# Attention and feed-forward kernel: probabilities × v in f32 for every pair of heads, and weight maxima spread over the partitions by a product with an identity

## The chip, the cores and the metric

One core of one Trainium2 chip. The metric is the device time of one execution in microseconds, of which the median over several runs is compared. TensorE is called PE here (PEld for its weight loads), VectorE DVE, ScalarE ACT, GpSimd POOL, and SP is the engine whose queue issues nearly all DMAs.

## What is computed

Shapes: 8 batches, 8 heads, 1152 keys, head dimension 64, 576 pooled queries; w_in 512×2048 and w_out 2048×512.

```python
def _attn_ref(q, k, v):
    q_pool = q.reshape(B, H, S // 2, 2, D).mean(axis=3)
    scores = scale * np.matmul(q_pool, k.transpose(0, 1, 3, 2))
    scores = scores - np.max(scores, axis=-1, keepdims=True)
    attn = np.exp(scores)
    attn = attn / (np.sum(attn, axis=-1, keepdims=True) + 1e-09)
    return np.matmul(attn, v).astype(np.float32)

def _moe_ref(x, w_in, w_out):       # x: 4608 x 512, heads side by side
    h = x @ w_in
    g = h * np.cos(h)
    return (g @ w_out).astype(np.float32)
```

q, k and v arrive as f32, the two weight matrices as f64.

## The kernel before

**Attention.** The work goes in 32 pairs of heads (`NP`; the pair number is `p` or `n`). Each pair has 9 key blocks of 128 keys (`KT`) and one remainder step, 10 units in all (`NU`). `s_unit` (L851, L871) makes the scores of a key block for both heads, 128 keys by 1024 queries, in the PSUM tile `st`, as f16 products in two parts. `soft` turns them into probabilities with one exponential on ACT. `av` and `av_mm` (L919) multiply these with v and add up in the PSUM tiles `ava` and `avb`, one for each head of the pair. The last 64 queries of both heads go through the remainder step, as products of half the array's width. The row maxima of the scores come from a product of its own (`mx`, L646 to L703), which DVE reduces (L656 and others), and the list `JOBS` loads, casts, splits and transposes q, k and v two pairs ahead of their use.

**Two ways of the product with v.** For `p < NDIR` (the first 4 pairs, which are batch 0) `soft` writes the probabilities as f32 into `pp` (L892), and `av` makes one f32 product for each of 4 query tiles and 2 heads, 8 products of 65 columns a key block. `prep_v` then writes v scaled as f32 (L768). For the other 28 pairs `soft` writes f32 `e` (L897), ACT casts it to f16 (L900), and POOL (L906) or, every third unit, DVE (L902) subtracts to get the low half; `prep_v` and `prep_v_lo` do the same to v (L772, L781). `av` then makes three products for one: high with high, high with low, low with high, 24 f16 products of 64 or 65 columns a key block. `prep_q1` casts the pooled q to f16 on ACT for `n < NDIR` (L592) and on DVE for the others (L594).

**Feed-forward.** A chunk is 256 rows. `ffn1` (L1149) and `ffn2` (L1205) do f16 products in three parts on PE; `evac`, `ew_group` and `evac2` do the cosine gate and the scaling on ACT, DVE and POOL. It starts when the weights of both layers are ready and is fed in between the attention units by a credit (`FRATE`); what is left runs after the last pair.

**Weights.** `weight_group` loads f64 columns as pairs of words (`wraw`), reduces their magnitude to one maximum a partition (`wmx`, L437), and puts f32 together (L444 to L450). The maximum over all partitions is reached by writing `wmx` to DRAM (L468, `row`), reading it back to every partition (L470, `wam`), and reducing on DVE (L477). A few small steps (L479 to L490) make a power of two of it, by which ACT and POOL scale and split the weights to f16 (L496 to L498). `weight_steps` moves the groups on, `SRATE` steps a unit.

**Order.** At the end `arrange` rebuilds the order of every engine's instructions with a list scheduler on cost estimates; each engine then runs its list strictly in that order. Matrix products of one PSUM tile are kept together as one node, to which an f32 product adds 0.3 us in its estimate.

Of the kernel before, what the change touches and what calls it, by code (L numbers as in the profile page):

```python
# [9 lines left out]
F32 = mybir.dt.float32  # L10
F16 = mybir.dt.float16
U32 = mybir.dt.uint32
I32 = mybir.dt.int32
AF = mybir.ActivationFunctionType
ALU = mybir.AluOpType
# [4 lines left out]
P = 128  # L20
POW2_MASK = 0x7F800000
POW2_HIGH = 0x40000000
TINY = 1e-12
PMAX = 2.0**6
MDIV = 64.0
VLAG = 3
# [5 lines left out]
NG = 8  # L32
# [3 lines left out]
DSH = 3  # L36
DFIRST = 0
WPOOL = 1
NDIR = 4
WLD = 2  # L40
WBN = 4
WGATE = 4
SRATE = 1.6
EWR = 2

_INS = ["q", "k", "v", "moe_w_in", "moe_w_out"]
# [80 lines left out]
def arrange(tc, nc, extra):  # L127
# [3 lines left out]
    for i in rec:  # L131
        rd, wr = boxes(i)
        eng = str(i.engine).split(".")[-1]
        if eng == "PE":
            key = wr[0][0].name
            if last_pe is not None and last_pe["key"] == key and len(last_pe["ins"]) < 12:
                nd = last_pe
            else:
                nd = last_pe = dict(eng=eng, ins=[], rd=[], wr=[], cost=0.0, lock=False, key=key)
                nd["tile"] = None  # L140
                nodes.append(nd)
            size = tuple(i.tile_size)
            c = max(n_out(wr) * 0.000421, 0.027)
            if rd[0][4] == 4:
                c = 0.3
            if size[0] == 64 and tuple(i.tile_position)[0] == 64:
                c = 0.0
            nd["cost"] += c
            nd["tile"] = size[0]
        else:  # L150
            nd = dict(eng=eng, ins=[], rd=[], wr=[], cost=0.0, lock=False)
            nodes.append(nd)
            if eng == "SP":
                nd["cost"] = 0.06
                nd["dma"], nd["lat"] = transfer(type(i).__name__, rd[0], wr[0])
            else:
                nd["cost"], nd["lock"] = estimate(i, type(i).__name__, rd, wr)
                nd["func"] = str(getattr(i, "func", "")) if eng == "Activation" else ""
        nd["ins"].append(i)
        nd["rd"] += rd  # L160
        nd["wr"] += wr
# [5 lines left out]
    for k, nd in enumerate(nodes):  # L167
        deps = set()
        for w, lst in ((0, nd["rd"]), (1, nd["wr"])):
            for t, box, *_ in lst:  # L170
                name = t.name
                if name not in hist:
                    hist[name] = ([], [], set())
                    tag = getattr(t, "tag", None)
# [72 lines left out]
    while total:  # L247
# [20 lines left out]
        c = nd["cost"]  # L268
# [43 lines left out]
def tile_attention_ffn(  # L312
# [87 lines left out]
    def all_max_end(dst, am):  # L400
        nc.vector.tensor_scalar_max(am, am, TINY)
        pow2_of(dst, am)

    w1v = w_in.rearrange("(c p) f -> p c f", p=P)
    w2v = w_out.rearrange("(f p) e -> p f e", p=P)

    w1_ready = [False]
    gate = [None]
    hsc_live = [0]

    def weight_group(wi, i0, fts):
        src, rows, width, dst = (
            (w1v, HP, DFF // NWP, w1),
            (w2v, NF, DM // NWP, w2),
        )[wi]
        n = len(fts)
        mx = sb2.tile([P, n], F32, tag="wmx", name="wmx")
        for a, ft in enumerate(fts):
            i = i0 + a
            cs = slice(i * width * WORDS, (i + 1) * width * WORDS)  # L420
            if wide:
                while hsc_live[0] >= 2:
                    yield
                hsc_live[0] += 1
                raw = sb2.tile([P, rows, width, 2], U32, tag="hsc", name="wraw")
                after(
                    nc.sync.dma_start(
                        raw.rearrange("p r w two -> p r (w two)"), src[:, :, cs]
                    ),
                    gate[0],  # L430
                )
                rv = raw.rearrange("p r w two -> p (r w) two")
                lo32, hi32 = rv[:, :, 0], rv[:, :, 1]
                fu = ft.bitcast(U32)
                for _ in range(WLD):
                    yield
                nc.vector.tensor_reduce(  # L437
                    mx[:, a : a + 1],
                    hi32.bitcast(F32),
                    axis=AX.X,  # L440
                    op=ALU.max,
                    apply_absolute_value=True,
                )
                nc.vector.tensor_scalar(  # L444
                    fu, hi32, 0x07FFFFFF, 3, ALU.bitwise_and, ALU.logical_shift_left
                )
                nc.vector.scalar_tensor_tensor(
                    fu, hi32, 0xC0000000, fu, ALU.bitwise_and, ALU.bitwise_or
                )
                nc.vector.scalar_tensor_tensor(  # L450
                    fu, lo32, 29, fu, ALU.logical_shift_right, ALU.bitwise_or
                )
                hsc_live[0] -= 1
            else:
                nc.sync.dma_start(
                    ft.rearrange("p (r w) -> p r w", r=rows), src[:, :, cs]
                )
                yield
                nc.vector.tensor_reduce(
                    mx[:, a : a + 1],  # L460
                    ft,
                    axis=AX.X,
                    op=ALU.max,
                    apply_absolute_value=True,
                )
            yield
        row = dram.tile([n, P], F32, tag="wrow", bufs=4, name="row")
        nc.sync.dma_start(row.rearrange("a p -> p a"), mx)  # L468
        am = sb2.tile([P, n, P], F32, tag="g", bufs=NG, name="wam")
        nc.sync.dma_start(  # L470
            am.rearrange("p a b -> p (a b)"),
            row.rearrange("a p -> (a p)").unsqueeze(0).broadcast_to([P, n * P]),
        )
        for _ in range(WBN):
            yield
        mw = sb2.tile([P, n], F32, tag="wmw", name="wmw")
        nc.vector.reduce_max(mw, am, axis=AX.X)  # L477
        if wide:
            nc.vector.tensor_scalar_max(mw, mw, 2.0**-15)  # L479
            mu = mw.bitcast(U32)  # L480
            ah = sb2.tile([P, n], U32, tag="wah", name="wah")
            nc.vector.tensor_scalar(ah, mu, POW2_HIGH, None, ALU.bitwise_and)
            nc.vector.tensor_scalar(
                mu, mu, 0x07FFFFFF, 3, ALU.bitwise_and, ALU.logical_shift_left
            )
            nc.vector.tensor_tensor(mu, mu, ah, ALU.bitwise_or)
        all_max_end(p2w[:, wi, i0 : i0 + n], mw)
        sc = sb2.tile([P, n], F32, tag="wsc", name="wsc")
        nc.vector.reciprocal(sc, p2w[:, wi, i0 : i0 + n])
        nc.vector.tensor_scalar_mul(sc, sc, 2.0**14)  # L490
        for a, ft in enumerate(fts):
            ds = slice((i0 + a) * width, (i0 + a + 1) * width)
            hi, lo = dst[0][:, :, ds], dst[1][:, :, ds]
            fv = ft.rearrange("p (r w) -> p r w", r=rows)
            if WPOOL:
                nc.scalar.activation(ft, ft, AF.Copy, scale=sc[:, a : a + 1])  # L496
                nc.scalar.copy(hi, fv)
                nc.gpsimd.tensor_sub(lo, fv, hi)  # L498
            else:
                nc.scalar.activation(hi, fv, AF.Copy, scale=sc[:, a : a + 1])  # L500
                nc.vector.scalar_tensor_tensor(
                    lo, fv, sc[:, a : a + 1], hi, ALU.mult, ALU.subtract
                )
            yield

    def weight_steps():
        stage = w2[1].rearrange("p f e -> p (f e)").bitcast(F32)
        live = []
        todo = [(wi, i) for wi in range(2) for i in range(0, NWP, 2)]
        done = 0  # L510
        while todo or live:
            if todo and len(live) < (2 if todo[0][0] == 0 else 1):
                wi, i = todo.pop(0)
                if wi == 0:
                    o = i % 4 * 1024
                    fts = [stage[:, o + a * 1024 : o + (a + 1) * 1024] for a in range(2)]
                else:
                    yt = sb1.tile([P, 2, 1024], F32, tag="y", name="wf")
                    fts = [yt[:, a] for a in range(2)]
                live.append(weight_group(wi, i, fts))  # L520
            for g in list(live):
                if next(g, 1) == 1:
                    live.remove(g)
                    done += 2
                    if done == NWP:
                        w1_ready[0] = True
                        nc.vector.reduce_max(w1max, p2w[:, 0, :], axis=AX.X)
                        rw = sb2.tile([P, 1], F32, tag="rw", name="rw")
                        nc.vector.reciprocal(rw, w1max)
                        nc.vector.tensor_scalar(  # L530
                            r1, p2w[:, 0, :], rw, 2.0**-24, ALU.mult, ALU.mult
                        )
            yield
# [868 lines left out]
```

## Time and profile before

| | |
|---|---|
| median of 3 runs | 1702.73 us (1696.87 to 1713.77) |
| profiled execution | 1703.86 us, of which the profile's span is 1702.1 us |
| mean granted PE clock | 0.953 |
| PE busy | 1548.4 us, 91% |
| ACT, DVE, POOL busy | 1216.5, 1134.9, 887.0 us (71%, 67%, 52%) |
| share of PE on the chain that ended last | 70% |

Busy times of different engines overlap, and a product's busy time counts its way through the array, so that consecutive products overlap each other: what a row of products costs PE is read from start to start in the timeline. `x8` behind a row is the number of records; an f32 product leaves two records, an f16 one leaves one.

### The profile page before, as it was taken

What the parts mean: (1) busy time and instruction counts of PE and PEld (TensorE: products, weight loads), DVE (VectorE), ACT (ScalarE), POOL (GpSimd) and SP (SyncE); (2) the same over time, 40 slices, a digit from 0 to 9 for tenths busy, and PEclk for the clock granted to TensorE, in tenths of its full rate; (3) what the DMA queues carried; (4) which work ended last, traced back from release to release, by engine and by line L of the source; (5) the groups of instructions that cost most, each with busy time, mean ns of one, the idle gap of its engine ahead of it and who ended that gap; (6) DMA issues with size and microseconds to landing.
All of it is one profiled execution on the core that took longest, in us unless ns stands there. A gap on an engine that the chain in (4) does not pass through costs nothing.

```text
span 1702.1 us, 39816 instructions
## 1 busy us (share of the span) xinstructions
PE 1548.4 (91%) x16728; PEld 999.9 (59%) x16728; DVE 1134.9 (67%) x1618; ACT 1216.5 (71%) x1476; POOL 887.0 (52%) x763
## 2 busy tenths in 40 slices
PE   2688877899899989998999999899999999997998
PEld 0465655566566546654666566666666666665664
DVE  6667668777776667676877767577777768632342
ACT  2244447888798868876887787798798879884442
POOL 3133227647647565756665556466756575461222
PEclk9687779899999999999999999999999999998999
DMA  9968875233643554354624324434444442101000
GB/s 203 185 117 138 161 142 94 66 69 81 101 79 73 98 99 85 79 105 78 111 59 99 84 52 105 78 72 97 101 78 87 88 112 47 34 21 27 13 25 20
DMA packets 339893, 147.34 MB, mean 87 GB/s; under 512 B 246016, under 2 KB 322816, under 8 KB 339712
## 3 DMA queue, kind: packets, MB, share of 16 engines
q1 hardware_dynamic: 339712, 144.79, 42.9%
q8 instruction: 131, 2.15, 0.6%
q14 instruction: 50, 0.41, 0.1%
HBM read 77.59 MB, written 10.51 MB: 52 GB/s over the span
## 4 chain that ended last, share of the span: by engine, by line
PE 70%; DVE 9%; DMA 8%; ACT 5%; issue 3%; POOL 2%; SPq 1%; another core or an unknown queue 0%; POOLq 0%; ACTq 0%; DVEq 0%
PE f L1205 21%; PE f L1149 19%; PE st L851 12%; PE ava L919 7%; PE avb L919 5%; PE mx L646 4%; DVE mxs L656 2%; DMA qld<-in_q_dram 2%; ACT e L897 2%; DMA am<-row 1%; POOL pp L906 1%; DMA wam<-row 1%; PE mx L686 1%; PE st L871 1%; DMA wraw<-in_moe_w_out_dram 1%
## 5 line engine op out<-in xcount | busy, mean ns | idle before, releaser
L906 POOL TENSOR_TENSOR pp<-e,pp 128x512 f16<-128x512 f32 x374 | 448.3, 1220 | 312.1 <-ACT pp L900 131.5
L1149 PE MATMUL f<-xT,w 128*128 128x256 f16 x3456 | 415.2, 277 | 15.7 <-DVE y L1175 8.9
L897 ACT ACTIVATE e<-st,eb 128x1024 f32<-128x1024 f32 x280 | 311.4, 1112 | 134.4 <-PE st L851 102.8
L656 DVE TENSOR_REDUCE mxs<-mx 128x2 f32<-128x1024 f32 x252 | 307.6, 1221 | 149.6 <-PE mx L646 147.9
L1205 PE MATMUL f<-w,g 128*128 128x512 f16 x1728 | 395.5, 380 | 0.0
L1149 PEld LDWEIGHTS <-w 128*128 128x128 f16 x3456 | 332.0, 99 | 88.0 <-issue 40.2
L900 ACT CAST pp<-e 128x1024 f16<-128x1024 f32 x280 | 292.5, 1044 | 8.9 <-PE ava L919 0.9
L919 PEld LDWEIGHTS <-pp 128*128 128x128 f16 (+1 forms) x7392 | 242.8, 101 | 71.0 <-issue 21.0
L1205 PEld LDWEIGHTS <-g 128*128 128x128 f16 x1728 | 161.2, 98 | 194.4 <-issue 14.5
L1114 POOL TENSOR_TENSOR g<-hsc,g 128x512 f16<-128x512 f32 x144 | 192.2, 1361 | 152.7 <-ACT g L1113 143.2
L919 PE MATMUL ava<-vc,pp 128*128 128x64 f16 (+4 forms) x4784 | 259.0, 205 | 13.2 <-POOL pp L906 10.9
L851 PE MATMUL st<-q1T,k 128*128 128x512 f16 x576 | 228.8, 397 | 14.1 <-ACT e L897 10.0
L851 PE MATMUL st<-q2T,k 128*128 128x512 f16 x576 | 229.1, 398 | 0.0
L919 PE MATMUL avb<-vc,pp 128*128 128x65 f16 (+1 forms) x3312 | 215.4, 205 | 2.6 <-POOL pp L906 2.6
L1175 DVE SCALAR_TENSOR_TENSOR y<-f,r1a,y 128x512 f32<-128x512 f32 x144 | 106.8, 746 | 115.1 <-ACT y L1174 113.6
L851 PEld LDWEIGHTS <-k 128*128 128x128 f16 x1152 | 103.7, 102 | 107.1 <-issue 34.1
L1171 ACT ACTIVATE hsc<-f,r 128x512 f32<-128x512 f32 x144 | 98.3, 684 | 80.5 <-PE f L1149 80.0
L1104 DVE TENSOR_TENSOR hsc<-hsc,y 128x512 f32<-128x512 f32 x144 | 128.5, 942 | 40.3 <-ACT y L1098 39.9
L579 POOL TENSOR_TENSOR kst<-kld,kst 128x512 f16<-128x512 f32 x64 | 88.9, 1390 | 127.0 <-ACT kst L578 119.9
L646 PE MATMUL mx<-k,q1T 64*128 64x512 f16 x504 | 105.8, 415 | 54.0 <-DVE mxs L656 25.8
L902 DVE TENSOR_TENSOR pp<-e,pp 128x1024 f16<-128x1024 f32 x93 | 127.6, 1372 | 37.9 <-ACT pp L900 37.5
L646 PEld LDWEIGHTS <-q1T 64*128 64x128 f16 x512 | 26.8, 94 | 163.1 <-issue 125.9
(113 smaller groups left out, 1561.8 us busy)
## 6 DMA issues: line engine op xcount, KB each, us to landing
vld<-in_v_dram SPq DMA_DIRECT2D x32, 576.0 KB
qld<-in_q_dram SPq DMA_DIRECT2D x64, 256.0 KB
kld<-in_k_dram SPq DMA_DIRECT2D x32, 320.0 KB
kld<-in_k_dram SPq DMA_DIRECT2D x32, 256.0 KB
wraw<-in_moe_w_in_dram SPq DMA_DIRECT2D x8, 1024.0 KB
wraw<-in_moe_w_out_dram SPq DMA_DIRECT2D x8, 1024.0 KB
out_dram<-ob SPq DMA_DIRECT2D x32, 256.0 KB
k<-k SPq DMA_DIRECT2D x64, 80.0 KB
```

The source lines that it names most:

```text
L646: nc.tensor.matmul(m[:, h, :], q1T[n][HALF[h], 2 * t + h, :], k1[n % 3][HALF[h], c * RB : (c + 1) * RB, h, :], start=True, stop=True, skip ...
L656: nc.vector.reduce_max(mxs[n][:, 2 * t : 2 * t + 2, c], m, axis=AX.X)
L851: nc.tensor.matmul(s[:, h, :].rearrange("p (t c) -> p t c", c=P), w[:, j, h, :], x[:, h : 2 * QT : 2, :], start=part == 0, stop=part == 1, ...
L897: nc.scalar.activation(e, s, AF.Exp, scale=exp_scale, bias=eb)
L900: nc.scalar.copy(pp[:, 0], e)
L902: nc.vector.tensor_sub(pp[:, 1], e, pp[:, 0])
L906: nc.gpsimd.tensor_sub(pp[:, 1, c], e[:, c], pp[:, 0, c])
L919: mm = nc.tensor.matmul(out, w, x, start=start, stop=False, skip_group_check=True)
L1104: nc.vector.tensor_mul(hj, hj, y[:, j : j + 2])
L1114: nc.gpsimd.tensor_sub(gt[:, 1], hj, gt[:, 0])
L1149: mm = nc.tensor.matmul(ps[:, fi, :], w1[wt][:, hp, fs], ck.xT[hp][:, xi, cs], start=n == 0, stop=n == 3 * HP - 1, skip_group_check=True,)
L1205: nc.tensor.matmul(po, gt[:, gi, f % 2, ts_], w2[wt][:, f, :], start=f == 0 and (gi, wt) == (0, 0), stop=f == NF - 1 and (gi, wt) == (1, 0),)
```

## The change

Four things are done. `NDIR` becomes 32, so all pairs take the f32 way, with the code that the first 4 pairs take now, and all casts of q go to ACT. The DRAM trip of the weight maxima is replaced by f32 products with an identity matrix into a PSUM tile with the tag of the feed-forward's `f`. The weights of the second layer go in groups of one column piece instead of two, two groups at a time instead of one. `SRATE` becomes 1.0 and the scheduler's estimate of an f32 product 0.112 us.

```diff
-NDIR = 4
+NDIR = 32
-SRATE = 1.6
+SRATE = 1.0
...
             if rd[0][4] == 4:
-                c = 0.3
+                c = 0.112
...
+    ident = sb2.tile([P, P], F32, tag="g", bufs=NG, name="ident")
+    nc.gpsimd.memset(ident, 0.0)
+    nc.gpsimd.affine_select(out=ident, in_=ident, compare_op=ALU.not_equal, fill=1.0,
...
-        row = dram.tile([n, P], F32, tag="wrow", bufs=4, name="row")
-        nc.sync.dma_start(row.rearrange("a p -> p a"), mx)
-        am = sb2.tile([P, n, P], F32, tag="g", bufs=NG, name="wam")
-        nc.sync.dma_start(
-            am.rearrange("p a b -> p (a b)"),
-            row.rearrange("a p -> (a p)").unsqueeze(0).broadcast_to([P, n * P]),
-        )
-        for _ in range(WBN):
-            yield
+        am = psum.tile([P, n, P], F32, tag="f", bufs=2, name="wam")
+        for a in range(n):
+            nc.tensor.matmul(
+                am[:, a, :],
+                mx[:, a : a + 1].broadcast_to([P, P]),
+                ident,
...
+        pw = p2w[:, wi, i0 : i0 + n]
         if wide:
-            nc.vector.tensor_scalar_max(mw, mw, 2.0**-15)
+            nc.vector.tensor_scalar_max(mw, mw, W64_MIN)
...
-            nc.vector.tensor_tensor(mu, mu, ah, ALU.bitwise_or)
-        all_max_end(p2w[:, wi, i0 : i0 + n], mw)
+            nc.vector.tensor_tensor(pw.bitcast(U32), mu, ah, ALU.bitwise_or)
+        else:
+            all_max_end(pw, mw)
...
-        todo = [(wi, i) for wi in range(2) for i in range(0, NWP, 2)]
+        todo = [(0, i) for i in range(0, NWP, 2)] + [(1, i) for i in range(NWP)]
...
-            if todo and len(live) < (2 if todo[0][0] == 0 else 1):
+            if todo and len(live) < 2:
```

How the order of the instructions moves, at three places. In these rows the number behind a name is that of the buffer. The lines of the changed kernel are 18 further down: L919 is L937 there, L646 is L664, L1149 is L1167.

PE, in the middle of the attention, before the change: the end of a key block's product with v (here into `avb`) and the scores that follow. Of the 24 pairs of a load and a product that make up the key block, the last two are shown.

```order
L919 LDWEIGHTS pp_12389
L919 MATMUL avb_12307<-vc_0_73,pp_12389 128x65
L919 LDWEIGHTS pp_12389
L919 MATMUL avb_12307<-vc_0_73,pp_12389 128x65
L851 LDWEIGHTS k1_0_98
L851 MATMUL st_12526<-q1T_10725,k1_0_98 128x512
L851 LDWEIGHTS k2_0_69
L851 MATMUL st_12526<-q2T_11667,k2_0_69 128x512
```

PE, at such a place after the change: whole key blocks of the product with v, two rows each, and the first rows of what follows (a `mx` product and scores).

```order
L937 MATMUL ava_8005<-vc_0_73,pp_8026 128x65 x4
L937 MATMUL avb_8055<-vc_0_73,pp_8026 128x65 x4
L704 LDWEIGHTS q1T_7613
L704 MATMUL mx_8049<-k1_2_105,q1T_7613 64x512
```

The 24 f16 products of a key block with their loads have become 8 f32 products, whose loads are part of the instruction. The rest of PE's order hardly moves: in both orders the first `ffn1` product stands after the scores of 42 of the 288 key blocks.

ACT, in the middle of the attention, before the change: exponentials (L897), casts to f16 (L900) and the feed-forward's evacuations (L1171, L1174).

```order
L897 ACTIVATE e_11973<-st_11913,eb_81 128x1024
L900 CAST pp_11975<-e_11973 128x1024
L1171 ACTIVATE hsc_11797<-f1_11870,r1_88 128x512
L1174 ACTIVATE y_11798<-f1_11870,r1a_89 128x512
L897 ACTIVATE e_12059<-st_11981,eb_81 128x1024
L900 CAST pp_12061<-e_12059 128x1024
```

ACT, at such a place after the change.

```order
L1189 ACTIVATE hsc_8808<-f1_8810,r1_88 128x512
L1192 ACTIVATE y_8809<-f1_8810,r1a_89 128x512
L910 ACTIVATE pp_8881<-st_8848,eb_81 128x1024
L610 CAST q1s_9142<-qld_9008 128x1152
L910 ACTIVATE pp_8927<-st_8883,eb_81 128x1024
```

The cast behind each exponential is gone, and once a pair the cast of the pooled q (L610), which stood on DVE, stands between two exponentials.

SP, while the weights are loaded, before the change: loads of q, k and weights, with a write (`row<-wmx`) and a read (`wam<-row`) of the maxima among them.

```order
L427 DMA wraw_611<-in_moe_w_in_dram 128x4x512
L600 DMA_TRANSPOSE q1T_382<-q1s_380 128x9x128
L628 DMA k2_0_69<-k1_2_100 64x4x128 x2
L470 DMA wam_477<-row_475 128x256
L621 DMA_TRANSPOSE k1_0_98<-kst_735 128x8x128
L550 DMA kld_776<-in_k_dram 128x2x320
L427 DMA wraw_661<-in_moe_w_in_dram 128x4x512
L468 DMA row_483<-wmx_364 128x2x1
```

PE, at the same stage after the change: the product of the maxima with the identity among products for the row maxima of the scores.

```order
L664 MATMUL mx_255<-k1_1_104,q1T_227 128x512
L482 MATMUL wam_524<-ident_98,wmx_331 128x128 x2
L664 LDWEIGHTS q1T_227
L664 MATMUL mx_261<-k1_1_104,q1T_227 128x512
```

The two DMAs of each of the 8 groups leave SP's queue, and 16 products (in 12 groups) enter PE's, each behind the DVE reduction that writes `wmx`.

More of the change, by code (lines that the diff above doesn't have):

```diff
@@ L23 @@
 TINY = 1e-12
+W64_MIN = 0.05859375
 PMAX = 2.0**6
@@ L405, in tile_attention_ffn @@
     w2v = w_out.rearrange("(f p) e -> p f e", p=P)
+    ident = sb2.tile([P, P], F32, tag="g", bufs=NG, name="ident")
+    nc.gpsimd.memset(ident, 0.0)
+    nc.gpsimd.affine_select(
+        out=ident,
+        in_=ident,
+        compare_op=ALU.not_equal,
+        fill=1.0,
+        base=0,
+        pattern=[[-1, P]],
+        channel_multiplier=1,
+    )
     w1_ready = [False]
@@ L466, in weight_group @@
             yield
-        row = dram.tile([n, P], F32, tag="wrow", bufs=4, name="row")
-        nc.sync.dma_start(row.rearrange("a p -> p a"), mx)
-        am = sb2.tile([P, n, P], F32, tag="g", bufs=NG, name="wam")
-        nc.sync.dma_start(
-            am.rearrange("p a b -> p (a b)"),
-            row.rearrange("a p -> (a p)").unsqueeze(0).broadcast_to([P, n * P]),
-        )
-        for _ in range(WBN):
-            yield
+        am = psum.tile([P, n, P], F32, tag="f", bufs=2, name="wam")
[4 more added lines that the diff above has]
+                ident,
+                start=True,
+                stop=True,
+                skip_group_check=True,
+            )
         mw = sb2.tile([P, n], F32, tag="wmw", name="wmw")
         nc.vector.reduce_max(mw, am, axis=AX.X)
+        pw = p2w[:, wi, i0 : i0 + n]
         if wide:
-            nc.vector.tensor_scalar_max(mw, mw, 2.0**-15)
+            nc.vector.tensor_scalar_max(mw, mw, W64_MIN)
             mu = mw.bitcast(U32)
@@ L483, in weight_group @@
             nc.vector.tensor_scalar(
-                mu, mu, 0x07FFFFFF, 3, ALU.bitwise_and, ALU.logical_shift_left
+                mu, mu, 0x07F00000, 3, ALU.bitwise_and, ALU.logical_shift_left
             )
-            nc.vector.tensor_tensor(mu, mu, ah, ALU.bitwise_or)
-        all_max_end(p2w[:, wi, i0 : i0 + n], mw)
+            nc.vector.tensor_tensor(pw.bitcast(U32), mu, ah, ALU.bitwise_or)
+        else:
+            all_max_end(pw, mw)
         sc = sb2.tile([P, n], F32, tag="wsc", name="wsc")
-        nc.vector.reciprocal(sc, p2w[:, wi, i0 : i0 + n])
+        nc.vector.reciprocal(sc, pw)
         nc.vector.tensor_scalar_mul(sc, sc, 2.0**14)
@@ L508, in weight_steps @@
         live = []
-        todo = [(wi, i) for wi in range(2) for i in range(0, NWP, 2)]
+        todo = [(0, i) for i in range(0, NWP, 2)] + [(1, i) for i in range(NWP)]
         done = 0
+        yt = None
         while todo or live:
-            if todo and len(live) < (2 if todo[0][0] == 0 else 1):
+            if todo and len(live) < 2:
                 wi, i = todo.pop(0)
@@ L517, in weight_steps @@
                 else:
-                    yt = sb1.tile([P, 2, 1024], F32, tag="y", name="wf")
-                    fts = [yt[:, a] for a in range(2)]
+                    if yt is None:
+                        yt = sb1.tile([P, 2, 1024], F32, tag="y", name="wf")
+                    fts = [yt[:, i % 2]]
                 live.append(weight_group(wi, i, fts))
@@ L523, in weight_steps @@
                     live.remove(g)
-                    done += 2
-                    if done == NWP:
+                    done += 1
+                    if done == NWP // 2:
                         w1_ready[0] = True
```

## The prediction

> **What bounds the kernel now.** First the busy times of the whole page, then the same cut into four stretches. Columns of the second view: start and end, length, then busy time (with the number of instructions) of PE, PEld, DVE, ACT and POOL, then the granted PE clock, the share of the DMA engines and GB/s.
>
> ```profile
> PE 1548.4 (91%) x16728; PEld 999.9 (59%) x16728; DVE 1134.9 (67%) x1618; ACT 1216.5 (71%) x1476; POOL 887.0 (52%) x763
> ```
>
> ```profile
> 0.00:260.00 260.00, 181.49 (x1218) 124.71 (x1218) 177.60 (x276) 103.54 (x119) 74.84 (x64) 0.81 0.82 155
> 260.00:300.00 40.00, 29.13 (x414) 18.72 (x413) 32.98 (x44) 26.94 (x30) 28.64 (x23) 0.93 0.58 104
> 300.00:1540.00 1240.00, 1193.07 (x14137) 762.60 (x14137) 871.75 (x1230) 1022.68 (x1241) 747.74 (x649) 0.98 0.40 80
> 1540.00:1702.00 162.00, 144.70 (x963) 93.90 (x961) 52.56 (x70) 63.37 (x90) 35.79 (x28) 0.94 0.08 21
> ```
>
> Three stages with different limits. Up to 260 us the weights come in: the DMA engines are 82% busy, PE only 70%, and its clock is cut to 0.81. These 260 us hold the four f32 pairs. From 300 to 1540 us attention and feed-forward run together, and PE is busy for 1193 of 1240 us, 96%, while ACT stands at 82%, DVE at 70% and POOL at 60%. After 1540 us only feed-forward is left, 162 us. So from 260 us on a microsecond more of PE work is a microsecond more of time, and a microsecond less on ACT, DVE or POOL is worth something only where PE waits for it. PE's idle time between 260 and 1540 us is 10.9 + 46.9 = 57.8 us. The clock lost another (1 - 0.93) × 40 + (1 - 0.98) × 1240 = 28 us there. These 86 us are all that relief of the other engines can bring.
>
> **The f32 product, the term that decides.** Timeline of PE, one key block of an f32 pair at full clock, then one of an f16 pair: start, length, operation, records. A stretch's cost is read from its start to the next stretch's start.
>
> ```profile
> 226.23 1.11 PE L919 MATMUL ava<-vc,pp 128*128 128x65 f32 x8
> 227.17 1.06 PE L919 MATMUL avb<-vc,pp 128*128 128x65 f32 x8
> 228.06 0.38 PE L851 MATMUL st<-q1T,k 128*128 128x512 f16 x1
> ```
>
> ```profile
> 1103.84 0.41 PE L919 MATMUL ava<-vc,pp 128*128 128x65 f16 x8
> 1104.09 0.41 PE L919 MATMUL avb<-vc,pp 128*128 128x65 f16 x8
> 1104.34 0.28 PE L919 MATMUL ava<-vc,pp 128*128 128x65 f16 x4
> 1104.46 0.29 PE L919 MATMUL avb<-vc,pp 128*128 128x65 f16 x4
> 1104.58 0.19 PE L871 MATMUL mx<-q1T,k 128*128 128x64 f16 x1
> ```
>
> Sixteen records (8 products) of f32 take 228.06 - 226.23 = 1.83 us, or 229 ns a product. The 24 f16 products take 1104.58 - 1103.84 = 0.74 us, or 31 ns each. A third as many products thus costs 2.5 times as much: 1.83 - 0.74 = 1.09 us more a key block. 28 pairs of 9 key blocks change over, 252 blocks: **+275 us**. I take the row at its full weight because the changed pairs run the very same branch of `av`, with the same shapes and tiles, as the four pairs that were measured.
>
> The remainder step adds a little. Groups of PE with the shapes kept apart (busy time, mean ns):
>
> ```profile
> L919 PE MATMUL ava<-vc,pp 128*64 128x65 f16 x896 | 28.7, 202 | 0.6 <-DVE rs L1010 0.4 <-DVE lx L1025 0.2
> ...
> L919 PE MATMUL ava<-vc,pp 128*64 128x65 f32 x128 | 6.0, 250 | 0.1
> ```
>
> The f16 row spans 28.7 / 28 = 1.0 us a pair (the 64-column products lie between its own), the f32 row 6.0 / 4 = 1.5 us. That is at most 0.5 × 28 = 13 us more, and at least nothing, since part of the f32 row fell into half clock. Nearest to the rows: **+8 us**.
>
> **The identity products.** Sixteen f32 products of 128 columns enter PE. None is in the trace. Nearest is the 65-column f32 product at 0.23 us, doubled at most for twice the columns: between 3.7 and 7.3 us, **+5 us**. What leaves is the DRAM trip, which the chain that ended last shows four times (start, length, what); with them stands a wait for a second-layer load:
>
> ```profile
> 92.59 8.69 DMA wam<-row
> ...
> 119.96 9.72 DMA row<-wmx
> 129.75 6.23 DMA wam<-row
> ...
> 146.45 4.12 DMA wam<-row
> ...
> 165.82 13.51 DMA wraw<-in_moe_w_out_dram
> ```
>
> The trips sum to 28.8 us, the most that can be gained. Two things speak against the whole of it: at 82% DMA load the next transfer is soon the late one, and the identity product makes PE itself wait for the DVE reduction of a weight piece, with the score products behind it. If PE stands for one late load as above, that costs 13.5 us. Between a gain of 28.8 and a loss of 13.5 I take **-15 us**, nearer the gain, because DVE already waits in order for the same loads, and PE for DVE, so this wait is mostly there today. The smaller weight groups and the slower pace balance: in both orders feed-forward starts after 42 of 288 key blocks. So the last stretch stays as it is, 162 us.
>
> **What is taken off the other engines.** From the page and from the groups by engine:
>
> ```profile
> L906 POOL TENSOR_TENSOR pp<-e,pp 128x512 f16<-128x512 f32 x374 | 448.3, 1220 | 312.1 <-ACT pp L900 131.5
> ...
> L900 ACT CAST pp<-e 128x1024 f16<-128x1024 f32 x280 | 292.5, 1044 | 8.9 <-PE ava L919 0.9
> ...
> L902 DVE TENSOR_TENSOR pp<-e,pp 128x1024 f16<-128x1024 f32 x93 | 127.6, 1372 | 37.9 <-ACT pp L900 37.5
> ```
>
> ```profile
> L781 DVE SCALAR_TENSOR_TENSOR vc<-vld,sv,vc 128x576 f16<-128x576 f32 x56 | 62.1, 1126 | 3.6 <-ACT vc L772 3.2
> ```
>
> 448 us leave POOL, 293 us ACT, 128 + 62 us DVE: over 900 us of work, none of it on the engine that bounds. Its worth is what PE waits there. PE's groups between 260 and 1540 us, the last column being idle time and its releasers:
>
> ```profile
> L919 PE MATMUL ava<-vc,pp 128*128 128x65 f16 (+2 forms) x4344 | 201.7, 196 | 11.3 <-POOL pp L906 9.8 <-DVE mxs L656 0.5 <-DVE rs L1010 0.4
> L851 PE MATMUL st<-q1T,k 128*128 128x512 f16 x500 | 192.6, 385 | 10.3 <-ACT e L897 10.0
> ...
> L646 PE MATMUL mx<-k,q1T 64*128 64x512 f16 x418 | 83.5, 396 | 19.6 <-ACT es L897 16.7 <-DVE mxs L656 2.9
> ```
>
> POOL's 9.8 us go with the instruction. ACT's 10.0 and 16.7 us should mostly go, as ACT loses over a quarter of its work and each unit gets a microsecond longer. Some clock comes back with the idle time. Of the 86 us I take half, **-45 us**, with ends at 0 and 86.
>
> One wait is new. The f16 cast of q moves from DVE to ACT:
>
> ```profile
> L594 DVE CAST q1s<-qld 128x1152 f16<-128x1152 f32 x28 | 37.7, 1347 | 24.8 <-POOL qld L585 24.7
> ```
>
> DVE stood 24.7 us in it, waiting for POOL's sum of q. On ACT the exponentials queue behind it, and PE's scores behind those. I count nothing, because that sum on POOL will no longer queue behind `pp`; without that cover it is up to 25 us.
>
> **Sum.** The profiled execution took 1703.9 us (1702.1 of span and 1.8 around it), the median of the runs shown is 1702.7, so the trace stands for the runs. 1703.9 + 275 + 8 + 5 - 15 - 45 = **1932 us**. A measurement of this kernel can't tell changes of under 1% from none.
>
> **Rivals.**
>
> *Nothing comes back.* PE fills no gap, and its clock gets worse. For the clock, look at PE after a gap in the f32 stage (the bracket gives the idle time before):
>
> ```profile
> 234.48 0.61 PE L646 MATMUL mx<-k,q1T 64*128 64x512 f16 x2 [5.39 <-DVE mxs L656]
> ...
> 240.87 1.97 PE L919 MATMUL ava<-vc,pp 128*128 128x65 f32 x8
> ...
> 246.72 1.18 PE L919 MATMUL ava<-vc,pp 128*128 128x65 f32 x8
> ```
>
> After 5.4 us of idleness PE works for 12 us without a gap before an f32 run of 8 shortens from 1.97 to 1.18 us. If f32 work holds the clock down like this everywhere, the 28 us of lost clock could double. 1704 + 275 + 13 + 7 + 28 = 2027 us with no relief at all; without the clock 1704 + 275 + 8 + 5 = 1992 us. Against it: from 300 us on feed-forward stands between the f32 runs. Chance 0.12.
>
> The Trainium skill ("TensorE: Matmul & The Clock Gate", "What's actually happening") says that the gate opens after about 3.4 us of sustained work. The trace differs here: 12 us passed. By the page the 28 us of lost clock would shrink rather than double, say to 14, an estimate that would put the sum at 1918 us.
>
> *All of it comes back.* The whole 86 us and the whole 28.8 us: 1704 + 275 + 0 + 4 - 115 = 1868 us. Chance 0.10.
>
> *The f32 weights load under other work, and the kernel gets faster.* An f32 product could cost what four f16 passes of its columns cost, 4 × 31 = 123 ns, if its weight loads ran ahead under the feed-forward products that surround it after 260 us. A key block then takes 8 × 123 ns = 0.99 us, and the change +0.25 × 252 = 63 us instead of 275. With my relief that gives 1720 us, with all relief 1704 + 63 + 13 - 115 = 1665 us, faster than before. It turns faster where a key block falls under 0.74 + (60 - 13) / 252 = 0.93 us with my relief. Against it: the runs of 8 at 226.23 and 227.17 us both take 0.9 us though f16 work stands directly ahead of them, so the loads of a run's later products are not hidden. Chance 0.04, half of it on either side of 1686 us.
>
> The Trainium skill ("FP8 and Floating Point Precision", "TensorE Precision Notes") gives true f32 as four passes through the array, which alone would be this rival's price. The row at 229 ns a product speaks against it, at nearly twice four passes.
>
> **How the numbers follow.** The forecast has 0.74 (about 1895 to 1975 us), the rivals 0.12, 0.10 and 0.04. All but the last are slower by 10% or more: slower 0.96, same 0.02, faster 0.02. The range reaches from the full relief, 1870, to beyond the case without any, where one of its doubtful costs (the cast on ACT, PE's wait for a weight load) also falls due: 1992 + 13.5 = 2005 us.
>
> **What the profile after would show.** PE busy for about 1830 us (1548 + 288, less some clock regained) and more than 96% of the middle stage; 1.8 us from the start of a key block's `ava` run to the start of the next work. No `pp` on POOL and DVE, ACT under 60%. A last stretch of about 160 us after the last f32 product. No `wam` DMA on the chain before 150 us. I am wrong if a key block of f32 in the middle takes well under 1.8 us at full clock, if the clock of the middle stage falls under 0.95, or if ACT's cast of q shows tens of microseconds of waits.

## The result and the profile after

The changed kernel takes 1908.22 us (median of 4 runs, 1897.34 to 1915.15) against 1704.78 us before: 1.119 times as long, 95% interval 1.1145 to 1.1235. The forecast was 1932 us with a range of 1870 to 2005. The profiled execution took 1903.45 us, with a span of 1901.3 us. That is 199.6 us more than the profiled execution before.

The page of the changed kernel, and the same four stretches (start and end, length, busy time of PE, PEld, DVE, ACT and POOL, granted clock, DMA share, GB/s):

```profile
PE 1788.7 (94%) x14240; PEld 1259.7 (66%) x14240; DVE 922.9 (49%) x1453; ACT 970.8 (51%) x1196; POOL 408.9 (22%) x361
```

```profile
0.00:260.00 260.00, 177.21 (x1284) 124.81 (x1286) 187.63 (x303) 112.35 (x127) 83.17 (x65) 0.81 0.67 154
260.00:300.00 40.00, 40.00 (x356) 32.19 (x353) 20.45 (x28) 23.68 (x28) 7.73 (x8) 0.98 0.41 84
300.00:1740.00 1440.00, 1426.04 (x11653) 1006.51 (x11652) 661.91 (x1053) 774.15 (x955) 286.73 (x265) 0.99 0.33 69
1740.00:1901.00 161.00, 145.50 (x958) 96.21 (x957) 52.96 (x71) 60.64 (x87) 31.31 (x24) 0.97 0.08 22
```

DVE, ACT and POOL fall to 49, 51 and 22%, and it brings little, because PE now has no room left: from 260 to 1740 us it is idle for 0 + 14 us, where it had 57.8 us. The clock loses (1 - 0.98) × 40 + (1 - 0.99) × 1440 = 15 us there, where it lost 28; it is printed to two places, so such a figure is good to some 7 us. So about 57 of the 86 us that were there to be had came back.

Where the extra time lies is read from two marks, the start of the first feed-forward product and that of the first one behind the last product with v. In PE's timeline before:

```profile
271.26 1.16 PE L1149 MATMUL f<-xT,w 128*128 128x256 f16 x9
...
1545.45 2.11 PE L1149 MATMUL f<-xT,w 128*128 128x256 f16 x9
```

After:

```profile
272.82 1.47 PE L1167 MATMUL f<-xT,w 128*128 128x256 f16 x12
...
1744.91 1.15 PE L1167 MATMUL f<-xT,w 128*128 128x256 f16 x9
```

Up to the first mark 272.82 - 271.26 = 1.6 us are added. Behind the second there is nothing: 1901.3 - 1744.9 = 156.4 us against 1702.1 - 1545.5 = 156.6. Between them it is 1472.1 against 1274.2 us: 197.9 of the 199.6 us lie in the attention that runs beside feed-forward.

One key block in the middle of the changed kernel (start, length, operation, records):

```profile
1000.81 1.00 PE L937 MATMUL ava<-vc,pp 128*128 128x65 f32 x8
1001.65 1.06 PE L937 MATMUL avb<-vc,pp 128*128 128x65 f32 x8
1002.54 0.38 PE L869 MATMUL st<-q1T,k 128*128 128x512 f16 x1
```

It takes 1.73 us: 0.84 for the first run of 8 records, 0.89 for the second. In the first stage before, where an `mx` product stood ahead of it, the first run took 0.94. Behind an `mx` product it still does in the changed kernel, so the neighbour makes the difference and not the stage:

```profile
1135.87 0.39 PE L664 MATMUL mx<-k,q1T 64*128 64x512 f16 x2
1136.19 1.11 PE L937 MATMUL ava<-vc,pp 128*128 128x65 f32 x8
1137.13 1.06 PE L937 MATMUL avb<-vc,pp 128*128 128x65 f32 x8
```

Against the f16 block's 0.74 us the difference is 0.99 us, not 1.09. The mean over all whole key blocks behind 300 us, taken from start to start without idle time, is 1.77 us in f32 and 0.78 us in f16: the same difference.

### The profile page after: what moved, and what is told of

Same layout as the page of the kernel before. It is cut to its first block, busy times and chain, and to the rows that moved or that the text cites. A ratio compares the mean times of both kernels' runs of the same rounds, so it can differ in the third digit from the quotient of the medians.

```text
span 1901.3 us, 33820 instructions
## 1 busy us (share of the span) xinstructions
PE 1788.7 (94%) x14240; PEld 1259.7 (66%) x14240; DVE 922.9 (49%) x1453; ACT 970.8 (51%) x1196; POOL 408.9 (22%) x361
## 4 chain that ended last, share of the span: by engine, by line
PE 87%; DVE 6%; DMA 4%; ACT 1%; issue 1%; SPq 1%; POOL 0%; ACTq 0%; POOLq 0%; DVEq 0%
PE f L1167 19%; PE f L1223 19%; PE ava L937 15%; PE avb L937 13%; PE st L869 13%; PE mx L664 4%; DVE mxs L674 2%; PE st L889 1%; DMA k<-kst 1%; PE mx L704 1%; DMA xT<-xs 1%; DMA q2T<-qs 1%; ACT pp L910 1%; PE mx L682 1%; DMA qld<-in_q_dram 0%
## 5 line engine op out<-in xcount | busy, mean ns | idle before, releaser
L910 ACT ACTIVATE pp<-st,eb 128x1024 f32<-128x1024 f32 x320 | 356.1, 1113 | 442.8 <-PE st L869 384.6
L1167 PE MATMUL f<-xT,w 128*128 128x256 f16 x3456 | 412.7, 276 | 11.6 <-DVE y L1193 7.0
L1167 PEld LDWEIGHTS <-w 128*128 128x128 f16 x3456 | 332.4, 99 | 82.6 <-issue 37.5
L937 PEld LDWEIGHTS ava<-vc,pp 128*128 128x128 f32 (+1 forms) x3328 | 331.3, 181 | 40.7 <-issue 19.1
L937 PE MATMUL ava<-vc,pp 128*128 128x65 f32 (+1 forms) x3328 | 343.4, 264 | 1.7 <-DVE lx L1043 1.6
L937 PE MATMUL avb<-vc,pp 128*128 128x65 f32 x2304 | 309.5, 278 | 0.0
L937 PEld LDWEIGHTS avb<-vc,pp 128*128 128x128 f32 x2304 | 285.8, 195 | 5.7 <-issue 4.3
L1132 POOL TENSOR_TENSOR g<-hsc,g 128x512 f16<-128x512 f32 x144 | 182.0, 1284 | 465.8 <-ACT g L1131 454.6
L597 POOL TENSOR_TENSOR kst<-kld,kst 128x512 f16<-128x512 f32 x64 | 83.2, 1299 | 586.2 <-ACT kst L596 581.6
L869 PEld LDWEIGHTS <-k 128*128 128x128 f16 x1152 | 111.4, 108 | 109.9 <-issue 40.1
L664 PE MATMUL mx<-k,q1T 64*128 64x512 f16 x504 | 104.4, 410 | 33.7 <-DVE mxs L674 24.5
L664 PEld LDWEIGHTS <-q1T 64*128 64x128 f16 x512 | 25.9, 94 | 145.4 <-issue 115.9
L1131 ACT CAST g<-hsc 128x512 f16<-128x512 f32 x144 | 84.2, 613 | 30.3 <-PE f L1223 29.5
L1192 ACT ACTIVATE y<-f,r1a 128x512 int32<-128x512 f32 x144 | 97.6, 681 | 3.2 <-DVE hsc L1122 3.2
```

The source lines that it names most:

```text
L664: nc.tensor.matmul(m[:, h, :], q1T[n][HALF[h], 2 * t + h, :], k1[n % 3][HALF[h], c * RB : (c + 1) * RB, h, :], start=True, stop=True, skip ...
L869: nc.tensor.matmul(s[:, h, :].rearrange("p (t c) -> p t c", c=P), w[:, j, h, :], x[:, h : 2 * QT : 2, :], start=part == 0, stop=part == 1, ...
L910: nc.scalar.activation(e, s, AF.Exp, scale=exp_scale, bias=eb)
L937: mm = nc.tensor.matmul(out, w, x, start=start, stop=False, skip_group_check=True)
L1132: nc.gpsimd.tensor_sub(gt[:, 1], hj, gt[:, 0])
L1167: mm = nc.tensor.matmul(ps[:, fi, :], w1[wt][:, hp, fs], ck.xT[hp][:, xi, cs], start=n == 0, stop=n == 3 * HP - 1, skip_group_check=True,)
```

## The experiments

Ratios are against the kernel before, run on the same chip beside each group. Its median there was 1718.5 to 1722.1 us, so ratios and not times are compared.

**NDIR back at 4, the rest of the change kept.**

```diff
-NDIR = 32
+NDIR = 4
```

> The changed kernel with NDIR back at 4: identity products, weight groups, pace and estimate stay, the f32 product of the other 28 pairs goes. Theory: the f32 product makes the whole difference, and the rest nothing, because the first feed-forward product started at 271 us before and 273 us after: 1700 to 1712 us, within 1% of before. Rival: the rest of the change gains the 15 us that the prediction counted, hidden under the product's cost: about 1690 us.

Measured: 0.9954 (0.9925 to 0.9983). The whole slowdown belongs to `NDIR`. The rest gains about 8 us, between the two forecasts, and this version is a little faster than both kernels.

**Half the pairs.**

```diff
-NDIR = 32
+NDIR = 18
```

> The changed kernel with NDIR = 18: 14 of the 28 pairs go over to f32. Theory: cost and relief belong to each pair, so half the change costs half: 1905 - 100 = 1805 us, give or take 12. Rival one: the relief is had as soon as some pairs leave ACT and POOL, and does not grow: 1704 + 14 x 9.3 - 63 = 1771 us. Rival two: it comes only when all pairs have left: 1704 + 14 x 9.3 = 1834 us.

Measured: 1.0459 (1.0412 to 1.0505), which is 79 us for 14 of 28 pairs. The theory's 1805 us would be 1.059, the first rival's 1771 us 1.039: the run lies between, and far from the second rival's 1834 us, 1.076. From the run with 4 pairs to this one a pair costs 0.0505 / 14 = 0.0036, from here to the full change (1.119) 0.0731 / 14 = 0.0052, so the first pairs to go over are the cheaper ones. In the trace PE's idle time of the middle lies between that before and that with all pairs over (windows of this run):

```profile
300.00:1640.00 1340.00, 1305.33 (x12944) 878.06 (x12944) 767.56 (x1145) 895.62 (x1095) 527.33 (x468) 0.99 0.37 74
```

35 us of 1340, with the clock already at 0.99. What the first pairs have ahead of the others is their place. In the kernel before, pairs 4 to 17 run up to about 900 us, and PE's idle time and the lost clock lie mostly there:

```profile
260.00:900.00 640.00, 594.33 (x7195) 383.06 (x7194) 463.96 (x649) 523.63 (x633) 394.29 (x344) 0.97 0.45 86
900.00:1540.00 640.00, 627.88 (x7359) 398.26 (x7357) 440.78 (x625) 525.99 (x637) 382.08 (x329) 0.99 0.36 76
```

The first half has 45.7 us of idle time and (1 - 0.97) × 640 = 19 us of lost clock to give back, the second 12.1 and 6 us. In this run the f32 pairs end at 982 us, and PE is idle for 10.5 us before and 24.2 us behind:

```profile
260.00:980.00 720.00, 709.52 (x5897) 507.83 (x5898) 346.10 (x545) 390.11 (x483) 150.97 (x143) 0.99 0.38 76
980.00:1640.00 660.00, 635.80 (x7402) 402.96 (x7400) 441.57 (x627) 529.44 (x641) 385.20 (x333) 0.99 0.37 73
```

So the relief belongs to the pairs that go over, as the theory has it, but it is not the same for each. Going over in another order was not tried.

**NDIR = 32 alone, in the kernel before.**

```diff
-NDIR = 4
+NDIR = 32
```

> The kernel before with NDIR = 32 and nothing else changed (DRAM trip, pace 1.6 and estimate 0.3 us stay). Theory: 1895 to 1915 us, as the full change. Rival: the scheduler's estimate of 0.3 us in place of 0.112, or the DRAM trip, costs time once PE is full: over 1925 us.

Measured: 1.1824 (1.1774 to 1.1874), or 2035 us. The rival holds: something else in the change gives back a third of what `NDIR` = 32 alone costs. The following three runs find it.

**The estimate put back to 0.3 us, in the changed kernel.**

```diff
-                c = 0.112
+                c = 0.3
```

> The changed kernel with the scheduler's estimate of an f32 product put back from 0.112 to 0.3 us, nothing else. NDIR = 32 alone took 1.1824 of the time before where the whole change takes 1.119. Theory: the estimate alone makes that difference, by placing loads and casts later against PE's real pace: 1.17 to 1.185 of the time before, with some 80 us of PE idleness in the middle and DMAs on the chain. Rival: the DRAM trip or the pace of the weights makes it: then this stays at 1.12 to 1.13.

Measured: 1.1611 (1.1574 to 1.1648). The scheduler's estimate alone is worth 0.042, about 72 us. No instruction differs, only the order. Windows of this run, and who waited for whom between 300 and 1820 us (in total, times, longest), ahead of the same two waits in the changed kernel between 300 and 1740 us:

```profile
300.00:1820.00 1520.00, 1443.77 (x11543) 1010.37 (x11542) 634.61 (x1036) 764.98 (x943) 275.45 (x262) 0.97 0.29 65
```

```profile
ACT kst L596 <- DMA k<-kst: 129.2, 36, 8.4
DVE amx L398 <- DMA am<-row: 128.7, 25, 7.8
```

```profile
ACT kst L596 <- DMA k<-kst: 48.6, 22, 5.4
...
DVE amx L398 <- DMA am<-row: 27.8, 11, 4.4
```

PE is idle for 76 us in the middle, where the changed kernel has 14, and the clock is at 0.97. ACT and DVE stand for 129 us each behind a DMA, against 49 and 28 us: ACT's cast of k writes a buffer (`kst`) that the DMA is still reading, and DVE's reduction needs what the DMA brings (`am`). PE stands behind them (its scores wait for ACT's exponential, `pp`; here between 300 and 1820 us):

```profile
L869 PE MATMUL st<-q1T,k 128*128 128x512 f16 x480 | 189.3, 394 | 47.3 <-ACT pp L910 47.3
```

In the changed kernel, between 260 and 1740 us, it is 9.5 us:

```profile
L869 PE MATMUL st<-q1T,k 128*128 128x512 f16 x498 | 190.4, 382 | 9.5 <-ACT pp L910 9.5
```

An f32 product of 0.229 us, counted as 0.3, makes the plan slower than the chip. That a DMA which the plan has ready in time therefore comes late is the reading that these waits fit; no run moved one transfer alone.

**The estimate at its true value.**

```diff
-                c = 0.112
+                c = 0.229
```

> The changed kernel with the estimate of an f32 product at 0.229 us, what the trace measured for it at full clock. Theory: the longer the estimate, the later loads and casts are placed against PE's real pace; 0.3 gave 1.161, 0.112 gave 1.119, so 0.229 lies between, 1.13 to 1.15. Rival: the best order is the one with true costs: 1.10 to 1.12.

Measured: 1.1300 (1.1254 to 1.1346), in order between 0.112 and 0.3. PE's idle time of the middle, 35 us, lies between 14 and 76 us too:

```profile
300.00:1775.00 1475.00, 1439.69 (x11614) 1012.78 (x11614) 641.86 (x1041) 769.31 (x945) 277.93 (x262) 0.98 0.32 67
```

What the trace measures is not the best number to plan this kernel with. By the same reading, a plan that is faster than the chip leaves transfers time in hand.

**The estimate of 0.112 us in the kernel before, with NDIR = 32.**

```diff
-NDIR = 4
+NDIR = 32
...
-                c = 0.3
+                c = 0.112
```

> The kernel before with NDIR = 32 and the estimate of 0.112 us; DRAM trip, pairs of second-layer pieces and pace 1.6 stay. With NDIR alone at 1.182, the full change at 1.119 and the full change with 0.3 at 1.161 it makes the square complete. Theory: both parts add, the weights part being worth about 0.02 under full PE load: 1.135 to 1.145. Rival: the weights part is worth what it was with NDIR = 4, 0.005: 1.12 to 1.13.

Measured: 1.1218 (1.1174 to 1.1261), the rival's value. With the new estimate the weights part can't be told from nothing (1.1218 against 1.119, intervals overlapping); with the old one it was worth 0.021 (1.1824 against 1.1611). The two do not add. Transfers less in SP's queue may count only where transfers come late; this was not tried by itself.

**Every PE cost in the plan times 0.6, for the f16 kernel.**

```diff
-NDIR = 32
+NDIR = 4
...
-            nd["cost"] += c
+            nd["cost"] += 0.6 * c
```

> NDIR = 4 with the rest of the change, and every PE cost in the scheduler's estimate multiplied by 0.6, so that loads, casts and transposes are placed earlier against PE's pace. Theory: what the estimate did for the f32 kernel it can do for this one: part of the 58 us of PE idleness and 28 us of lost clock in the middle goes, 0.97 to 0.99 of the time before. Rival: the waits in the f16 kernel come from POOL and ACT being full, which no order cures, or the earlier loads only crowd them: 0.995 to 1.03.

Measured: 1.0683 (1.0651 to 1.0714), slower than either forecast, where the same kernel with its costs as they were took 0.9954. Windows of this run:

```profile
300.00:1660.00 1360.00, 1224.76 (x14169) 790.64 (x14168) 892.06 (x1232) 1015.43 (x1234) 750.81 (x649) 0.97 0.35 74
```

PE is idle for 135 us in the middle. Where POOL, DVE and ACT are 55 to 75% busy, a plan that thinks PE faster than it is leaves PE waiting for them: by the groups of the whole run PE's scores stand for 29.8 us for ACT's `e`, and its `mx` products for 49.4 us for DVE's `mxs`:

```profile
L869 PE MATMUL st<-q1T,k 128*128 128x512 f16 x576 | 229.9, 399 | 42.5 <-ACT e L915 29.8 <-ACT pp L910 11.8
...
L664 PE MATMUL mx<-k,q1T 64*128 64x512 f16 x504 | 107.8, 421 | 73.9 <-DVE mxs L674 49.4 <-ACT es L915 7.9 <-DMA q1T<-q1s 7.5
```

An error in the same direction helped the f32 kernel, in which those engines have room; there it stood on one kind of product, here on all of them, so that the room decides is argued and not shown.

**Two PE estimates moved towards the trace, for the f16 kernel.**

```diff
-            c = max(n_out(wr) * 0.000421, 0.027)
+            c = max(n_out(wr) * 0.000421, 0.031)
...
-                c = 0.0
+                c = 0.000225 * n_out(wr)
```

> NDIR = 4 with the rest of the change, and two PE estimates moved towards the trace: at least 0.031 us a product (0.027 so far), and 0.000225 us a column for the second of two products that share the array by halves of its rows (0 so far; the trace has 0.33 us for two of 512 columns, the estimate 0.216). Shrinking all PE estimates to 0.6 gave 1.068, so the other direction may gain: 0.975 to 0.99. Rival: the estimates are at their best, or noise of the order decides: 0.995 to 1.02.

Measured: 1.0061 (1.0035 to 1.0086), about 1% slower than without the edit (0.9954). The rival holds; whether the estimates were at their best or the order is chance is not parted.

**Each f32 product split in two.** The same columns are streamed, the weights loaded twice.

```diff
-                    mm = av_mm(acc[h][:, t, :], pp[:, c : c + P], vf[p % 2][:, h, j], start)
+                    mm = av_mm(acc[h][:, t, 0:33], pp[:, c : c + P], vf[p % 2][:, h, j, 0:33], start)
...
+                    mm = av_mm(
+                        acc[h][:, t, 33:65], pp[:, c : c + P], vf[p % 2][:, h, j, 33:65], False
+                    )
```

> The changed kernel with every full-width f32 product made as two, of 33 and 32 columns, with the same weights: the same columns stream, the weights are loaded twice. It parts the 111 ns of a record into load and stream. Theory: the load (about 53 ns by the difference between a run of 0.84 and one of 0.89 us) is not hidden, so each of the 2304 products takes two more loads: 2304 x 0.106 = 245 us more, 2150 us. Rival: the columns stream for all of the 111 ns and the loads lie beneath: no change beyond some 20 us, 1905 to 1930 us.

Measured: 1.576 (1.5678 to 1.5842), 2717 us, three times the cost that the theory gave. PE's timeline in the middle, and two windows of the same run:

```profile
1001.20 1.87 PE L937 MATMUL ava<-vc,pp 128*128 128x33 f32 x16
1002.90 1.95 PE L937 MATMUL avb<-vc,pp 128*128 128x33 f32 x16
1004.69 0.38 PE L869 MATMUL st<-q1T,k 128*128 128x512 f16 x1
```

```profile
1100.00:1200.00 100.00, 100.00 (x791) 76.08 (x788) 33.22 (x62) 40.54 (x55) 16.93 (x15) 0.88 0.24 50
...
1300.00:1400.00 100.00, 100.00 (x683) 76.95 (x682) 27.12 (x46) 27.26 (x33) 10.12 (x11) 0.80 0.23 54
```

Twice the records take twice the time, 3.49 against 1.73 us, though each streams half the columns: 105 to 112 ns a record at 32, 33 and 65 columns. Both forecasts fall. The price is not a load of 53 ns with the stream behind it; the stream does not show in it at all. That explains 288 × 1.76 = 507 us of the (1.576 - 1.119) × 1722 = 787 us. The rest is of the size of the lost clock: these windows show PE busy without a gap at a clock of 0.88 and 0.80, and over the whole middle (1 - 0.85) × 2040 = 306 us are lost:

```profile
260.00:2300.00 2040.00, 2026.36 (x14756) 1525.30 (x14755) 681.12 (x1096) 754.25 (x922) 293.76 (x270) 0.85 0.24 53
```

**Each f32 product twice as wide.**

```diff
-                    mm = av_mm(acc[h][:, t, :], pp[:, c : c + P], vf[p % 2][:, h, j], start)
+                    mm = av_mm(
+                        acc[h].rearrange("p t d -> p (t d)")[
+                            :, t * (D + 1) : t * (D + 1) + 2 * (D + 1)
+                        ]
...
+                        pp[:, c : c + P],
+                        vf[p % 2][:, h, min(j, KT - 2) : min(j, KT - 2) + 2].rearrange(
+                            "p j d -> p (j d)"
+                        ),
```

> The changed kernel with the full-width f32 products streaming 130 columns instead of 65 against the same weights (the sums of neighbouring query tiles run into each other, so the output is another; number and size of the weight loads are unchanged). Theory from the split run, where records of 33 and 32 columns took as long as one of 65: a record's 107 to 111 ns is its weight load alone, and the stream lies beneath. Twice the columns then still fit: 108 ns at 2.4 columns a ns twice over, run of 8 at 0.85 to 0.95 us, time within 2% of the changed kernel. Rival: load and stream follow each other, 53 + 58 ns: a record grows to about 165 ns, a run of 8 to 1.3 us, 250 us more.

This kernel adds neighbouring query tiles into each other and does not compute the attention; it serves for the time alone. Measured in one execution: 1907.6 us, 1.110 times the median before of its group, within 1% of the changed kernel's 1.119. PE's timeline:

```profile
1002.07 1.06 PE L937 MATMUL ava<-vc,pp 128*128 128x130 f32 x8
1002.96 1.06 PE L937 MATMUL avb<-vc,pp 128*128 128x130 f32 x8
1003.86 0.38 PE L869 MATMUL st<-q1T,k 128*128 128x512 f16 x1
```

Runs of 8 take 0.89 and 0.90 us with 130 columns, against 0.84 and 0.89 with 65. The stream lies beneath the load up to twice the width of this kernel.

That the price is the load, and not a fixed one of each record, is read from the remainder step of the changed kernel. Its f32 products hold 64 weight columns (`128*64`) and stream the same 65 columns:

```profile
311.30 1.16 PE L937 MATMUL ava<-vc,pp 128*64 128x65 f32 x32
312.28 0.29 PE L937 MATMUL ava<-vc,pps 128*64 128x65 f32 x4
312.50 0.39 PE L869 MATMUL st<-q1T,k 128*128 128x512 f16 x1
```

The 32 records take 0.98 us. At a fixed 105 ns they would take 3.4 us, and 1.7 us if they all ran in pairs, one on each half of the array; in pairs it is 61 ns a pair, near half of 105 to 112 ns for half the weight columns.

The Trainium skill ("TensorE: Matmul & The Clock Gate", "Weight-path perf modes — Fast Weight Load (FWL) and DoubleRow") says that the fast way of loading weights is off for f32 inputs, and ("LDWEIGHTS (loading the stationary operand)") gives a load as its columns / 1.2 in ns, for 128 columns an estimate of 107 ns. The records here, 105 to 112 ns, agree.

**The cast of q back on DVE.**

```diff
-        if n < NDIR:
+        if n < 4:
             nc.scalar.copy(q1s, src)
```

> The changed kernel with the cast of q back on DVE for all but the first 4 pairs. In the changed kernel ACT stands 44.6 us before this cast. Theory: that costs nothing, since PE is idle for only some 14 us between 260 and 1740 us: within 1% of the changed kernel, 1.11 to 1.13 of before. Rival: the exponentials queued behind the cast are among what PE waits for, and 10 to 20 us come back: 1.105 to 1.11.

Measured: 1.1194 (1.116 to 1.1228), the changed kernel's value. ACT's 44.6 us before that cast cost nothing that can be measured.

**No f32 pair at all.**

```diff
-NDIR = 32
+NDIR = 0
```

> The changed kernel with NDIR = 0: the first 4 pairs go the f16 way too. Theory: an f32 pair costs only where PE is the bound; in the first 260 us it is 70% busy, so the 39 us of PE work that leave (36 key blocks by 1.09 us) bring little, and the casts that come in load ACT, DVE and POOL: 0.99 to 1.01 of the time before (NDIR = 4 with the rest of the change gave 0.995). Rival: PE's half clock there makes it the bound after all: 0.965 to 0.98.

Measured: 1.0042 (1.0018 to 1.0065), against 0.9954 with the first 4 pairs in f32. In the first stage the f32 way is worth 0.009, about 15 us, although PE is busy for 35 us more with it there. Windows of this run, then of the run with 4 pairs:

```profile
0.00:260.00 260.00, 131.59 (x1510) 75.65 (x1510) 224.94 (x298) 134.16 (x149) 147.74 (x117) 0.78 0.70 147
...
0.00:260.00 260.00, 166.47 (x1246) 117.41 (x1247) 186.97 (x300) 110.72 (x124) 85.07 (x70) 0.83 0.69 153
```

Without f32 pairs PE falls from 166 us to 132 of 260, and DVE rises from 187 to 225: there DVE is the engine with the least room, and the f32 way is the cheap one.

## Why the prediction was right

Direction and size held; the forecast is 24 us above the median. Term by term:

| Term | Forecast | Measured | From |
|---|---|---|---|
| f32 key blocks | +275 | +250 | 252 × (1.73 - 0.74) |
| remainder step | +8 | +6 | see below |
| identity products and DRAM trip | +5 - 15 | +2 | first feed-forward product at 272.8 instead of 271.3 us |
| relief of PE | -45 | -57 | idle 57.8 to 14.0, lost clock 28 to 15 us |
| profiled execution | 1932 | 1903.5 | the terms sum to 1905 |

For the remainder step, PE's timeline before (the f32 rows stand above, with the experiment on the width):

```profile
366.67 0.96 PE L919 MATMUL ava<-vc,pp 128*64 128x65 f16 x48
367.45 0.27 PE L919 MATMUL ava<-vc,pps 128*64 128x65 f16 x6
367.66 0.40 PE L664 MATMUL mx<-k,q1T 64*128 64x128 f16 x8
```

From start to start it takes 0.99 us in f16 and 1.20 us in f32: 28 × 0.21 = 6 us. The prediction worked this term out from busy times, which do not show what a row costs, and left out the second row (`pps`); that its 8 us lies near 6 is luck.

That the sum lies within 2% of the measured time is in part luck as well: the f32 term was 25 us too large, the relief 12 us too small, and the DRAM trip brought 12 us less than it was given.

*The deciding term was sound, and a tenth too large.* The row was taken from the first stage, where the first run of a block took 0.94 us behind an `mx` product; behind a feed-forward product it takes 0.84. The difference is about one record's time; why the neighbour matters was not tried.

*The DRAM trip was sized wrongly.* 28.8 us of trips on the chain became no earlier start of feed-forward: the profiled start moved by +1.6 us, and the 8 us of the run with NDIR = 4 are all that the rest of the change brings. On the chain up to 300 us the trips (`wam` and `row`, 9.5% of it before) are gone, and PE's products with v stand for 30% of it where they stood for 14%: other work that was nearly as late took their place. A transfer on the chain is not a sum to be taken off when such work runs beside it.

*The relief was half forecast, by a wrong road.* ACT's and POOL's lighter load was given as its reason. The runs show a condition that the prediction passed over: with the estimate at 0.3 us the same light load leaves 76 us of idleness, more than before the change. So that the relief came out near the forecast is luck: it needs the order that 0.112 makes. The edit stood in the section on the change, and the prediction gave it no price; it was worth 0.042 to 0.061, or 70 to 105 us, more than any other term but the product itself.

*The rivals.* The case with nothing coming back gave 1992 us; with the old estimate it would have been the truth (1.161 to 1.182). The rival on the faster side, loads that run ahead beneath other work, is refuted, and turned round: the stream hides beneath the load. Four passes of 31 ns was the wrong thing to count. The clock did not worsen in the middle (0.98 before, 0.99 after), as the feed-forward between the runs suggested. The cast on ACT was rightly put at nothing. The waits that the prediction named as a sign of being wrong did appear, 44.6 us before the cast, but the run with the cast back on DVE shows that they cost nothing: PE had no idle time for them to lengthen.

## What to carry to other kernels

An f32 product with 128 weight columns costs two weight loads, 0.22 us, whether it streams 32 or 130 columns: before trading f16 parts for f32, put the wide side on the stream, and use f32 where PE has room (here the first stage, worth 15 us) and not where PE is the bound. When a kernel's order comes from a planner, an edit to one of its costs is a term of the sum like any other: price it. Count a relieved engine only as far as PE's idle time and lost clock go.

## What the runs showed of the hardware

PE's clock can fall without idleness. In the split run PE is busy for 100.0 of 100 us at a clock of 0.80. Taken from start to start, the f32 products with v stand for 55 of these 100 us, for 44 of those at 0.88, and for 39 of a third window of this run, at full clock:

```profile
1500.00:1600.00 100.00, 99.23 (x788) 70.41 (x787) 37.24 (x62) 42.42 (x55) 15.96 (x14) 1.00 0.23 57
```

In the changed kernel, where f32 takes 1.73 of some 6 us a block (1472.1 us over about 250 blocks), the clock stays at 0.99. In the kernel before, behind the gap of 5.4 us that the prediction shows, an f32 block takes 3.5 of the 5.9 us to the next one:

```profile
240.87 1.97 PE L919 MATMUL ava<-vc,pp 128*128 128x65 f32 x8
242.63 1.91 PE L919 MATMUL avb<-vc,pp 128*128 128x65 f32 x8
244.34 0.63 PE L851 MATMUL st<-q1T,k 128*128 128x512 f16 x1
...
246.72 1.18 PE L919 MATMUL ava<-vc,pp 128*128 128x65 f32 x8
```

So in these stretches the clock is low where the share of f32 is large. The Trainium skill ("TensorE: Matmul & The Clock Gate", "Why this matters for your kernels") explains a fall of the clock by idle gaps of over 3 us; the split run had none in those windows. That the f32 loads are the cause, and from which share on, was not tried.
